# A spectral block with its gradients: the ScalarE order of one backward stage written down, two kinds of loads moved in their queue

## The chip, the cores and the metric

The kernel runs on one core of a Trainium2 chip. The metric is the device time of one execution in microseconds. A core has five engines that each run their own instructions in order: PE (TensorE, matrix products), DVE (VectorE), ACT (ScalarE), POOL (GpSimd) and SP (SyncE, which here only issues transfers). PEld is the loading of weights into PE. Transfers are issued by SP, by POOL, and run on 16 DMA engines that all issuers share.

## The reference

The forward pass takes x (2048 rows of 576 columns, bfloat16) and a condition c:

- six vectors `sa, ca, ga, sb, cb, gb` are cut from `silu(c) @ w_mod`;
- `h = layernorm(x) * (1 + ca) + sa`; `y = irfft2(rfft2(h) * (w_r + i w_i))`; `x1 = x + ga * y`;
- `h2 = layernorm(x1) * (1 + cb) + sb`; `out = x1 + gb * (((h2 @ w_gate) * (h2 @ w_up)) @ w_down)`, with 4608 hidden columns.

The outputs are `out` and the gradients of `sum(out * grad_out)` by x, w_r, w_i, w_gate, w_up, w_down, c and w_mod.

## The kernel before

Rows are dealt to 16 tiles of 128, hidden columns to 36 blocks of 128. The forward transform, the filter and the inverse transform come first, then one long loop over the 36 blocks that makes the products `g` and `u`, the gradient that flows back into `h2` (summed in `acc`) and the weight gradients. A weight gradient of one block and one half of the columns is a chain of 16 matmuls `u57p` (line 638) that ACT copies into `so` (line 640). The change lies behind this loop, in four stretches of the program:

- **The norm stage** (lines 940 to 1034), 16 tiles in four steps that overlap from tile to tile. `t1_norm` loads `n2c` and `yc` on SP, and by `norm_back` (lines 859 to 872) puts the gradient through the second layernorm: ACT makes `u` (line 862), DVE makes `w` from `n2c` (line 864) and the small sums `ab`, adds the residual to `u` (line 867) and gets `gxr` (line 872), `gxa` and `gxf` (lines 978 to 980). POOL stores `gxr`. `t1_turn` turns `gxf` on PE (line 985; called the turn below) and adds five column and diagonal sums that read `n2c` and `yc`, which frees these buffers. `t1_cols` and `t1_rows` are two more products each. ACT copies their results: `gyT` (line 987), `zt` (line 1005) and `b_Vp` (line 1013). These five results of a tile share three PSUM buffers.
- **The second stage** (lines 1119 to 1165), 19 groups of frequencies, with the filter gradients on DVE.
- **The third stage** (lines 1171 to 1225), 16 tiles: inverse transform and the first layernorm's backward, again by `norm_back`.
- **The output projection**, 1152 matmuls `u3p` (line 1269) of hidden activations `hl` with `w_down` (held in `wd0` to `wd4`). Rows go in eight pairs of tiles. A pair needs four loads `hl` of 576 KB, numbered 0 to 31 over all pairs. Their buffers are six slots in turn, except for numbers 24 to 27 (pair 6), which have a pool `hlp` of their own that is laid where the third stage's buffers were. Behind tiles 8 to 13 stands a `section` each (line 922): a vector is spread by PE (`spp`, line 913), copied and scaled by ACT (`dmb`, `o8`, lines 925 and 932), `wmj` is loaded and `o8` stored on SP, and DVE takes five products `pr7` (line 938).

**What sets the order.** The library orders each engine's instructions by priorities and by what it expects to be ready, and places waits where data or buffers ask for them. Two tools overrule it: `in_order` chains instructions of one engine, and `tc.issue_after` (through `behind`) puts one behind another. `deal` (line 874) writes PE's order from the end of the long loop to the end of the third stage. It puts the pieces of the three stages in a row, and after each piece some fillers out of one list: the last 144 weight gradient products (`held`), then the `u3p` products of the first five pairs (`proj`, 720 of them). A step of the norm stage gets 16 fillers, of the second stage 12, of the third stage 20 in its first step and then 16. ACT's order in these stages isn't written down. SP's order in the norm stage is written in part (lines 1023 to 1026): the late stores of weight gradients stand behind chosen loads of `n2c`.

SP issues in its order. A transfer that waits holds all later ones of SP.

Of the kernel before, what the change touches and what calls it, by code (L numbers as in the profile page):

```python
# [10 lines left out]
BF = mybir.dt.bfloat16  # L11
# [8 lines left out]
NT = 16  # L20
S = 2048
D = 576
DP = 640
# [75 lines left out]
def build(ctx, tc, A_x, A_w_r, A_w_i, B_w_gate, B_w_up, B_w_down, c_in, w_mod, grad_out,  # L99
# [50 lines left out]

    def pe_since(mark):
        return [i for i in nc.cur_bb.bb.instructions[mark:] if i.engine == mybir.EngineType.PE]

    def in_order(seq):

# [422 lines left out]
    with ExitStack() as ms:  # L578
# [17 lines left out]
        with ExitStack() as bs:  # L596
# [31 lines left out]
            def u57_items(sf, rhs_n, done):  # L628
                so = so4[:, nso[0] % NSO, :]
                nso[0] += 1  # L630
                items = []
                for h in range(2):
                    pw = []

                    def item(h, t, pw=pw):
                        if t == 0:
                            pw.append(u57ps.tile([128, 512], FP32, name="u57p", tag="x"))
                        mm = nc.tensor.matmul(pw[0][:, 0:288], lhsT=sf[:, t, :], rhs=rhs_n(t, h * 288, 288), start=(t == 0), stop=(t == NT - 1))  # L638
                        if t == NT - 1:
                            nc.scalar.copy(so[:, h * 288:(h + 1) * 288], pw[0][:, 0:288])  # L640
# [164 lines left out]
    with ExitStack() as ts:  # L805
# [47 lines left out]
        def behind(insts):  # L853
# [2 lines left out]
                es.enter_context(tc.issue_after(i_))  # L856
            return es

        def norm_back(pool, gn, n, rstd, res, out, name):
            s12 = pool.tile([128, 2], FP32, name="s12" + name)  # L860
            u = pool.tile([128, D], BF, name="u" + name)
            nc.scalar.activation(out=u[:], in_=gn[:], func=ACT.Copy, scale=rstd, accum_out=s12[:, 0:1])
            w = pool.tile([128, D], BF, name="w" + name, bufs=1)
            nc.vector.scalar_tensor_tensor(out=w[:], in0=gn[:], scalar=rstd, in1=n, op0=MUL, op1=MUL, accum_out=s12[:, 1:2])  # L864
            ab = pool.tile([128, 2], FP32, name="ab" + name)
            nc.vector.tensor_scalar(out=ab[:], in0=s12[:], scalar1=-1.0 / D, scalar2=None, op0=MUL)
            nc.vector.tensor_tensor(out=u[:], in0=u[:], in1=res, op=ADD)
            if name == "1":
                nc.scalar.activation(out=w[:], in_=n, func=ACT.Identity, bias=ab[:, 0:1], scale=ab[:, 1:2])  # L869
            else:  # L870
                nc.vector.tensor_scalar(out=w[:], in0=n, scalar1=ab[:, 1:2], scalar2=ab[:, 0:1], op0=MUL, op1=ADD)
            return nc.vector.tensor_tensor(out=out, in0=u[:], in1=w[:], op=ADD)
# [12 lines left out]
        def wide(m):  # L885
            return slice(m * 128, (m + 1) * 128)
# [53 lines left out]
        with ExitStack() as r1:  # L940
# [3 lines left out]
            csA = ps_cs.tile([128, 512], FP32, name="csA")  # L944
            csB = ps_cs.tile([128, 512], FP32, name="csB")
            csC = ps_cs.tile([128, 512], FP32, name="csC")
            rings = {k: c1b.tile([128, n, DP], BF, name=k) for k, n in (("gxr", 4), ("gxf", 2))}
            ga_h = c1b.tile([128, D], BF, name="ga_h")
            gxa = c1b.tile([128, D + 4], BF, name="gxa")
            with tc.high_priority(HEAD_START):  # L950
                for k in rings:
                    nc.vector.memset(rings[k][:, :, D:DP], 0.0)
                nc.vector.memset(gxa[:, D:D + 4], 0.0)
            ld, gyTs, zts = {"order": []}, {}, {}

            def t1_norm(t):
                if t == 0:
                    nc.sync.dma_start(ga_h[:], modb_d[:, MGA, :])
                for k, src in (("n2c", n2_d), ("yc", y_d)):
                    ld[k, t] = c1.tile([128, D], BF, name=k, bufs=5 if k == "n2c" else 4)  # L960
                    with behind(ld["order"]):
                        ins = nc.sync.dma_start(ld[k, t][:], src[:, t, :])
                    ld[k, "ins", t] = ins.ins
                if t in (1, 2):
# [12 lines left out]
                gf = rings["gxf"][:, t % 2, :]  # L977
                nc.vector.tensor_tensor(out=gxa[:, 0:D], in0=gx, in1=ga_h[:], op=MUL)
                nc.vector.tensor_tensor(out=gf[:, 0:DF], in0=gxa[:, 0:DF], in1=gxa[:, D:DF - 2:-1], op=ADD)
                nc.vector.tensor_tensor(out=gf[:, DF:D], in0=gxa[:, 1:DF - 1], in1=gxa[:, D - 1:DF - 1:-1], op=SUB)  # L980

            def t1_turn(t):
                pt = ps_fp.tile([128, 5, 128], BF, name="trp", tag="fp")
                for m in range(5):
                    nc.tensor.transpose(pt[:, m, :], rings["gxf"][:, t % 2, wide(m)], ident[:])
                gyTs[t] = c1z.tile([128, 5, 128], BF, name="gyT")
                nc.scalar.copy(gyTs[t][:], pt[:])
# [11 lines left out]
            def t1_cols(t):  # L999
                zt = zts[t] = c1z.tile([128, 2, FP], BF, name="zt")  # L1000
                for cc in range(2):
                    zp = ps_fp.tile([128, 512], FP32, name="zp", tag="fp")
                    for m in range(3):
                        nc.tensor.matmul(zp[:, :FP], lhsT=gyTs[t][:, 2 * cc + m, :], rhs=T["RF"][:, 3 * cc + m, :], start=(m == 0), stop=(m == 2))
                    nc.scalar.copy(zt[:, cc, :], zp[:, :FP])

            def t1_rows(t):
                zt = zts[t]
                for cc in range(2):
                    vp = ps_fp.tile([128, 512], FP32, name="vp", tag="fp")  # L1010
                    nc.tensor.matmul(vp[:, :FP], lhsT=T["G1"][:, t, 0, :], rhs=zt[:, cc, :], start=True, stop=False)
                    nc.tensor.matmul(vp[:, :FP], lhsT=T["G1"][:, t, 2 if cc == 0 else 1, :], rhs=zt[:, 1 - cc, :], start=False, stop=True)
                    nc.scalar.copy(Vv[:, :, t, cc, :], vp[:, :FP].rearrange("k (g f) -> k g f", f=4))

            steps = [t1_norm, t1_turn, t1_cols, t1_rows]
            for k in range(NT + len(steps) - 1):
# [230 lines left out]
        late = {8: (MSB, of_sums(dsb)), 9: (MCB, of_rows(dcb)), 10: (MGA, of_rows(dga)), 11: (MGB, of_rows(dgb)), 12: (MSA, of_sums(dsa)), 13: (MCA, of_rows(dca))}  # L1247


        proj = []  # L1250
        for tp_ in range(NT // 2):
            hls = [first_hl[q] if tp_ == 0 else hl_load(4 * tp_ + q, behind_=ld["yc", "ins", NT - 1]) for q in range(4)]
            x1t = o2p.tile([128, 2, D], BF, name="x1t3")
            with behind([last[nc.gpsimd]] if tp_ == 0 else []):
                x1l = nc.gpsimd.dma_start(x1t[:], x1_d[:, 2 * tp_:2 * tp_ + 2, :])
# [3 lines left out]
            for group in [[(0, 0), (1, 0)], [(0, 1), (1, 1)]] if tp_ == 0 else [[(0, 0)], [(0, 1)], [(1, 0)], [(1, 1)]]:  # L1259
# [5 lines left out]
                        obs[ti] = o2p.tile([128, D], BF, name="ob3", bufs=4)  # L1265
                for fb in range(NFB):
                    f0, w = wd_part(fb)
                    for ti, h in group:
                        mm = nc.tensor.matmul(p2[ti][:, 0:288], lhsT=hls[fb // 9][:, fb % 9, ti * 128:(ti + 1) * 128], rhs=w[:, fb - f0, h * 288:(h + 1) * 288], start=(fb == 0), stop=(fb == NFB - 1))  # L1269
                for ti, h in group:  # L1270
                    nc.scalar.copy(obs[ti][:, h * 288:(h + 1) * 288], p2[ti][:, 0:288])
# [90 lines left out]
```

## Time and profile before

| what | value |
|---|---|
| median of three runs | 1550.34 us (1549.38 to 1552.56) |
| the profiled execution, and its span | 1548.15 us, 1546.4 us |
| PE, DVE, ACT, POOL busy | 97%, 69%, 38%, 15% of the span |
| end of the long loop and first norm tiles, 1254 to 1275 us | PE busy 18.11 of 21.00 us, DVE 20.91 |
| norm stage, 1275.00 to 1324.12 us | PE busy 38.65 of 49.12 us, DVE 34.09, ACT 27.81, granted clock 0.97 |
| rest of it, 1324.12 to 1348 us | PE busy 23.88 of 23.88 us |
| second stage, 1348 to 1404 us | PE busy 56.00 of 56.00 us, DVE 48.53, ACT 45.85 |
| third stage, 1404 to 1470.4 us | PE busy 66.13 of 66.40 us, DVE 53.37, ACT 45.31 |

Start and end times of matmuls are modelled, so "busy" says that PE had work, not that it worked at its peak. The granted clock is the share of its full rate that PE was given. A row of a timeline gives the start, the length, the engine, the line, the operation with its tiles, and how many were merged; behind it, in brackets, how long the engine had idled and what ended that. A group of n merged matmuls lasts n spacings and the length of the last one. T1 is below the start of the turn of tile 1, and so on; S is the end of PE's part in the third stage.

### The profile page before, as it was taken

How to read it: one execution, taken by the hardware profiler on the slowest of the kernel's cores; microseconds unless marked ns; L12 is line 12 of the kernel's file. 1: busy time of each engine (PE TensorE's matmuls, PEld its weight loads, DVE VectorE, ACT ScalarE, POOL GpSimd, SP SyncE). 2: the span in 40 equal slices, each digit the busy share in tenths (PEclk: the TensorE clock that was granted, in tenths of full speed). 3: DMA queues.
4: the chain of work that ended last, by engine and by line, in shares of the span. 5: the costliest groups of instructions: out<-in, count | busy, mean ns of one | idle time of the engine just before them, and what ended most of it. 6: DMA issues, size and time to landing. Idle time of an engine off the chain costs nothing.

```text
span 1546.4 us, 29006 instructions
## 1 busy us (share of the span) xinstructions
PE 1495.4 (97%) x11144; PEld 1013.4 (66%) x11144; DVE 1060.0 (69%) x2647; ACT 582.4 (38%) x1189; POOL 237.2 (15%) x360
## 2 busy tenths in 40 slices
PE   6999989999999999999999999999999997999987
PEld 4666533566666666666676666766667665888765
DVE  6866643666667766677676676766767686488883
ACT  6667732322222222222222222222222225586752
POOL 0001212111101111111110110211111022221022
PEclk9999999999999999999999999999999999999999
DMA  8968997587868768778687686876877688856685
GB/s 315 286 202 226 263 269 216 141 171 151 180 122 167 148 123 165 148 149 170 121 165 149 142 158 139 155 168 128 163 143 147 120 207 237 275 186 195 191 296 156
DMA packets 487181, 280.42 MB, mean 181 GB/s; under 512 B 408865, under 2 KB 457378, under 8 KB 486018
## 3 DMA queue, kind: packets, MB, share of 16 engines
q1 hardware_dynamic: 458882, 175.32, 54.4%
q0 software_dynamic: 28160, 103.25, 23.0%
q8 instruction: 87, 1.43, 0.4%
q14 instruction: 52, 0.43, 0.1%
HBM read 108.62 MB, written 82.31 MB: 123 GB/s over the span
## 4 chain that ended last, share of the span: by engine, by line
PE 83%; DVE 8%; DMA 4%; ACT 3%; issue 2%; SPq 0%; POOL 0%; POOLq 0%; DVEq 0%; ACTq 0%
PE u57p L638 26%; PE u8p L741 18%; PE gup L705 16%; PE u4p L446 7%; PE u3p L1269 5%; PE gup L700 3%; DMA xc<-in_A_x_dram 2%; DVE w L864 1%; DMA n2c<-n_d 1%; DMA hl<-hhT_d 1%; PE zp L385 1%; DVE ln_st L176 1%; ACT w L869 1%; PE u4p L441 1%; DVE goT L417 1%
## 5 line engine op out<-in xcount | busy, mean ns | idle before, releaser
L746 DVE TENSOR_TENSOR acc<-acc,u8p 128x288 f32<-128x288 f32 (+1 forms) x1088 | 483.0, 452 | 276.4 <-PE u8p L741 272.8
L741 PE MATMUL u8p<-wT,ggT 128*128 128x288 bf16 x1152 | 328.4, 287 | 2.9 <-DVE acc L746 2.9
L741 PE MATMUL u8p<-wT,guT 128*128 128x288 bf16 x1152 | 328.0, 286 | 0.0
L705 PE MATMUL gup<-h2T,wgu 128*128 128x512 bf16 x1152 | 298.0, 380 | 0.0
L640 ACT CAST so<-u57p 128x288 bf16<-128x288 f32 x216 | 85.9, 398 | 519.1 <-PE u57p L638 511.7
L638 PE MATMUL u57p<-h2p,gu_sf 128*128 128x288 bf16 x1152 | 187.0, 287 | 0.0
L638 PE MATMUL u57p<-h2p,gg_sf 128*128 128x288 bf16 x1152 | 186.0, 286 | 0.0
L1269 PE MATMUL u3p<-wd,hl 128*128 128x288 bf16 x1152 | 172.2, 293 | 7.7 <-DMA hl<-hhT_d 6.9
L705 PEld LDWEIGHTS <-wgu 128*128 128x128 bf16 x1152 | 109.4, 98 | 98.0 <-issue 17.1
L741 PEld LDWEIGHTS <-ggT 128*128 128x128 bf16 x1152 | 112.4, 98 | 66.7 <-issue 14.0
L446 PE MATMUL u4p<-goT,wdT 128*128 128x512 bf16 x656 | 151.3, 380 | 3.2 <-DVE ghh_st L168 2.6
L741 PEld LDWEIGHTS <-guT 128*128 128x128 bf16 x1152 | 112.6, 98 | 58.9 <-issue 3.6
L707 ACT CAST gT<-gup 128x512 bf16<-128x512 f32 x144 | 84.3, 585 | 131.6 <-PE gup L705 129.7
L1269 PEld LDWEIGHTS <-hl 128*128 128x128 bf16 x1152 | 109.1, 100 | 36.1 <-DMA hl<-hhT_d 7.9
L638 PEld LDWEIGHTS <-gu_sf 128*128 128x128 bf16 x1152 | 112.5, 98 | 28.9
L638 PEld LDWEIGHTS <-hh_sf 128*128 128x128 bf16 x1152 | 112.6, 98 | 28.5
L638 PEld LDWEIGHTS <-gg_sf 128*128 128x128 bf16 x1152 | 112.3, 98 | 28.4
L707 ACT CAST uT<-gup 128x512 bf16<-128x512 f32 x144 | 84.3, 586 | 77.6 <-PE gup L705 77.6
L446 PEld LDWEIGHTS <-wdT 128*128 128x128 bf16 x656 | 61.2, 98 | 75.5 <-issue 10.2
L638 PE MATMUL u57p<-gonC,hh_sf 128*128 128x288 bf16 x576 | 99.7, 286 | 0.0
L718 POOL DMA_DIRECT2D hhT_d<-hhT x36 | 33.2, 922 | 375.4 <-DVE hhT L709 352.6
L168 DVE CAST ghh_st<-u4p 128x512 bf16<-128x512 f32 x56 | 38.7, 690 | 59.1 <-PE u4p L446 59.0
(373 smaller groups left out, 1839.9 us busy)
## 6 DMA issues: line engine op xcount, KB each, us to landing
ghhT_d<-ghh_st POOLq DMA_DIRECT2D x36, 512.0 KB, 4.0
ghh<-ghhT_d POOLq DMA_DIRECT2D x36, 512.0 KB, 7.9
hhT_d<-hhT POOLq DMA_DIRECT2D x36, 512.0 KB, 6.3
hl<-hhT_d SPq DMA_DIRECT2D x28, 576.0 KB, 5.7
out_dram<-woT SPq DMA_DIRECT2D x70, 128.0 KB, 2.0
wdn<-in_B_w_down_dram SPq DMA_DIRECT2D x18, 288.0 KB, 3.8
wd<-in_B_w_down_dram POOLq DMA_DIRECT2D x36, 144.0 KB, 4.9
out_dram<-so SPq DMA_DIRECT2D x36, 144.0 KB, 2.8
```

Of the source, the lines that this page charges most:

```text
L168: nc.vector.tensor_copy(dst, src)
L176: nc.vector.bn_stats(out=st[:, t, h, :], in_=xt[:, t, h * 288:(h + 1) * 288])
L446: nc.tensor.matmul(pt[:], lhsT=wdTs[k][:, j, m, :], rhs=goT[:, 4 * sb4:4 * sb4 + 4, m, :], start=(m == 0 and n == 5), stop=(m == n - 1))
L638: mm = nc.tensor.matmul(pw[0][:, 0:288], lhsT=sf[:, t, :], rhs=rhs_n(t, h * 288, 288), start=(t == 0), stop=(t == NT - 1))
L640: nc.scalar.copy(so[:, h * 288:(h + 1) * 288], pw[0][:, 0:288])
L700: nc.tensor.matmul(pts[-1][:], lhsT=wgu[r, 8, jw * 128:(jw + 1) * 128], rhs=h2T[r, 4 * sb4:4 * sb4 + 4, 4, :], start=True, stop=False)
L705: nc.tensor.matmul(pts[k][:], lhsT=wgu[:, 4 * wi_ + m, jw * 128:(jw + 1) * 128], rhs=h2T[:, ts_, m, :], start=False, stop=(m == 3))
L707: nc.scalar.copy((gT, uT)[wi_][:, th_, :], pts[k][:])
L718: nc.gpsimd.dma_start(hhT_d[:, :, fb, :].rearrange("tp f x -> f tp x"), hhT[:].rearrange("f (tp ti) p -> f tp (ti p)", ti=2))
L741: nc.tensor.matmul(pu[:, 0:288], lhsT=l_, rhs=r_, start=(k == 0), stop=(k == len(mms) - 1))
L746: summed[t] = nc.vector.tensor_tensor(out=ghb(t)[:, hs_] if fbs[-1] == NFB - 1 else dst, in0=dst, in1=pu[:, 0:288], op=ADD).ins
L1269: mm = nc.tensor.matmul(p2[ti][:, 0:288], lhsT=hls[fb // 9][:, fb % 9, ti * 128:(ti + 1) * 128], rhs=w[:, fb - f0, h * 288:(h + 1) * 288], ...
```

## The change

1. **ACT's order in the norm stage.** `followed` notes for a matmul which ACT copy evacuates it. While `deal` writes PE's order, it also lists ACT's copies of the norm stage and of the fillers in it, in the order of their matmuls, and puts the `u` of tile k+2 at the end of step k (the turn of step k is that of tile k-1). `in_order` then chains them. So `u` of tile t stands behind the copy `gyT` of tile t-3, and, while weight gradient fillers last, behind that step's `so`. Before, the library had it behind `gyT` of tile t-6.
2. **Loads.** `n2c` is asked for one tile further ahead than `yc`; `yc` has three buffers for four. SP's order keeps its shape: `n2c` of tile t is still the load that waits for the turn of tile t-5; beside it stands now `yc` of tile t-2 where `yc` of tile t-1 stood.
3. **Buffers.** `gxf` has a ring of three for two, `gxr` loses its padding (and its memset goes), `gb_h` gets a pool of its own between `wd4` and the last left slot of `hl`. Addresses behind it move by 1152 bytes.
4. **Third stage.** 14 fillers for 16 in each step but the first.
5. **Last pairs.** The loads `hl` of pairs 5 and 6 are asked for with those of pair 4, and those of pair 7 in two halves with pairs 5 and 6. SP's order in the built program: 22 and 23 at the third stage's end, 24 to 27 right behind, all ahead of the sections' transfers; 28 and 29 behind the second section's stores, 30 and 31 behind the fourth's. Before, 24 stood behind the first section's stores, 25 to 27 behind the fourth section's load, 28 and 29 behind the sixth's, 30 and 31 behind the fifth's stores.

PE's order is the same up to the third stage. There it has 244 fillers instead of 272, and the 28 come behind the stage. DVE's order in the norm stage becomes regular (a tile's `gxa` and `gxf` directly behind the next tile's `w`), and in the last stretch the filter gradients come ahead of all `pr7`. POOL loads `wd4` ahead of the store of `gxr` 11 instead of behind it.

```diff
+    then_act = {}
+
+    def followed(mm, act):
+        then_act[mm.ins.name] = act.ins
...
-                            nc.scalar.copy(so[:, h * 288:(h + 1) * 288], pw[0][:, 0:288])
+                            followed(mm, nc.scalar.copy(so[:, h * 288:(h + 1) * 288], pw[0][:, 0:288]))
...
         wd_pool(28, 8)
+        gbhp = pool("gbhp", 1)
         hl_pool("left", ts)
...
-            nc.scalar.activation(out=u[:], in_=gn[:], func=ACT.Copy, scale=rstd, accum_out=s12[:, 0:1])
+            scaled[name].append(nc.scalar.activation(out=u[:], in_=gn[:], func=ACT.Copy, scale=rstd, accum_out=s12[:, 0:1]).ins)
...
         def deal(held, proj):
-            more, seq = held + proj, list(lead)
+            more, seq, acts = held + proj, list(lead), scaled["2"][0:3]
             for n, (stage, k, ins) in enumerate(staged):
+                last_ = len(seq)
                 seq += ins
                 steps = sum(x[:2] == (stage, k) for x in staged)
                 at = sum(x[:2] == (stage, k) for x in staged[:n + 1])
-                q = 16 if stage == 1 else 12 if stage == 2 else 20 if k == 0 else 16
+                q = 16 if stage == 1 else 12 if stage == 2 else 20 if k == 0 else 14
                 q = q * at // steps - q * (at - 1) // steps
                 seq, more = seq + more[:q], more[q:]
+                if stage == 1:
+                    acts += [then_act[i_.name] for i_ in seq[last_:] if i_.name in then_act]
+                    acts += scaled["2"][k + 2:k + 3] * (at == steps and k > 0)
             in_order(seq)
+            in_order(acts)
...
-            rings = {k: c1b.tile([128, n, DP], BF, name=k) for k, n in (("gxr", 4), ("gxf", 2))}
+            rings = {k: c1b.tile([128, n, w], BF, name=k) for k, n, w in (("gxr", 4, D), ("gxf", 3, DP))}
...
-                for k, src in (("n2c", n2_d), ("yc", y_d)):
-                    ld[k, t] = c1.tile([128, D], BF, name=k, bufs=5 if k == "n2c" else 4)
+                for k, src, tt in [("n2c", n2_d, 0)] * (t == 0) + [("n2c", n2_d, t + 1)] * (t < NT - 1) + [("yc", y_d, t)]:
+                    ld[k, tt] = c1.tile([128, D], BF, name=k, bufs=5 if k == "n2c" else 3)
                     with behind(ld["order"]):
-                        ins = nc.sync.dma_start(ld[k, t][:], src[:, t, :])
-                    ld[k, "ins", t] = ins.ins
+                        ins = nc.sync.dma_start(ld[k, tt][:], src[:, tt, :])
+                    ld[k, "ins", tt] = ins.ins
...
-            gb_h = modh(MGB, "gb_h", tl, nc.gpsimd)
+            gb_h = modh(MGB, "gb_h", gbhp, nc.gpsimd)
...
-        proj = []
+        proj, hls_of = [], {0: first_hl}
         for tp_ in range(NT // 2):
-            hls = [first_hl[q] if tp_ == 0 else hl_load(4 * tp_ + q, behind_=ld["yc", "ins", NT - 1]) for q in range(4)]
+            for nq in {4: range(16, 28), 5: (28, 29), 6: (30, 31)}.get(tp_, range(4 * tp_, 4 * tp_ + 4) if 0 < tp_ < 4 else ()):
+                hls_of.setdefault(nq // 4, []).append(hl_load(nq, behind_=ld["yc", "ins", NT - 1]))
+            hls = hls_of[tp_]
```

The copies of `gyT`, `zt`, `b_Vp` and of the projection's results are wrapped in `followed` in the same way as that of `so`.

More of the change, by code (lines that the diff above doesn't have):

```diff
@@ L857, in behind @@
             return es
+        scaled = {"1": [], "2": []}
         def norm_back(pool, gn, n, rstd, res, out, name):
@@ L950, in build @@
             with tc.high_priority(HEAD_START):
-                for k in rings:
-                    nc.vector.memset(rings[k][:, :, D:DP], 0.0)
+                nc.vector.memset(rings["gxf"][:, :, D:DP], 0.0)
                 nc.vector.memset(gxa[:, D:D + 4], 0.0)
@@ L976, in t1_norm @@
                 ld["gx", t] = nc.gpsimd.dma_start(gx1_d[:, t, :], gx).ins
-                gf = rings["gxf"][:, t % 2, :]
+                gf = rings["gxf"][:, t % 3, :]
                 nc.vector.tensor_tensor(out=gxa[:, 0:D], in0=gx, in1=ga_h[:], op=MUL)
@@ L984, in t1_turn @@
                 for m in range(5):
-                    nc.tensor.transpose(pt[:, m, :], rings["gxf"][:, t % 2, wide(m)], ident[:])
+                    mm = nc.tensor.transpose(pt[:, m, :], rings["gxf"][:, t % 3, wide(m)], ident[:])
                 gyTs[t] = c1z.tile([128, 5, 128], BF, name="gyT")
-                nc.scalar.copy(gyTs[t][:], pt[:])
+                followed(mm, nc.scalar.copy(gyTs[t][:], pt[:]))
                 gh, gx = ghb(t), rings["gxr"][:, t % 4, :]
@@ L1003, in t1_cols @@
                     for m in range(3):
-                        nc.tensor.matmul(zp[:, :FP], lhsT=gyTs[t][:, 2 * cc + m, :], rhs=T["RF"][:, 3 * cc + m, :], start=(m == 0), stop=(m == 2))
-                    nc.scalar.copy(zt[:, cc, :], zp[:, :FP])
+                        mm = nc.tensor.matmul(zp[:, :FP], lhsT=gyTs[t][:, 2 * cc + m, :], rhs=T["RF"][:, 3 * cc + m, :], start=(m == 0), stop=(m == 2))
+                    followed(mm, nc.scalar.copy(zt[:, cc, :], zp[:, :FP]))
             def t1_rows(t):
@@ L1011, in t1_rows @@
                     nc.tensor.matmul(vp[:, :FP], lhsT=T["G1"][:, t, 0, :], rhs=zt[:, cc, :], start=True, stop=False)
-                    nc.tensor.matmul(vp[:, :FP], lhsT=T["G1"][:, t, 2 if cc == 0 else 1, :], rhs=zt[:, 1 - cc, :], start=False, stop=True)
-                    nc.scalar.copy(Vv[:, :, t, cc, :], vp[:, :FP].rearrange("k (g f) -> k g f", f=4))
+                    mm = nc.tensor.matmul(vp[:, :FP], lhsT=T["G1"][:, t, 2 if cc == 0 else 1, :], rhs=zt[:, 1 - cc, :], start=False, stop=True)
+                    followed(mm, nc.scalar.copy(Vv[:, :, t, cc, :], vp[:, :FP].rearrange("k (g f) -> k g f", f=4)))
             steps = [t1_norm, t1_turn, t1_cols, t1_rows]
@@ L1267, in build @@
                     f0, w = wd_part(fb)
+                    mms = []
                     for ti, h in group:
                         mm = nc.tensor.matmul(p2[ti][:, 0:288], lhsT=hls[fb // 9][:, fb % 9, ti * 128:(ti + 1) * 128], rhs=w[:, fb - f0, h * 288:(h + 1) * 288], start=(fb == 0), stop=(fb == NFB - 1))
-                for ti, h in group:
-                    nc.scalar.copy(obs[ti][:, h * 288:(h + 1) * 288], p2[ti][:, 0:288])
+                        mms.append(mm)
+                for (ti, h), mm in zip(group, mms):
+                    followed(mm, nc.scalar.copy(obs[ti][:, h * 288:(h + 1) * 288], p2[ti][:, 0:288]))
                 proj += pe_since(mark) if tp_ < 5 else []
```

## The prediction

> **What bounds the kernel now.** I read the busy shares first, then the windows of the four stretches behind the long loop, then PE's waits there, and then the timelines of the engines that the waits name.
>
> ```profile
> PE zp L1004 <- ACT b_Vp L1013: 8.6, 5, 3.3
> PE u3p L1269 <- DMA hl<-hhT_d: 6.9, 3, 4.0
> ```
>
> PE is the bound almost everywhere, so only what PE loses counts. The waits (us, times, longest) from 1272 us on name two losses: `zp` in the norm stage waits 8.6 us for ACT's copy `b_Vp`, and `u3p` behind the stages waits 6.9 us for `hl`. The first, step by step from PE's timeline (starts of the turns T1, T5, T6, T8, T10, T11):
>
> ```profile
> 1272.69 0.44 PE L985 MATMUL trp<-ident,gxf 128*128 128x128 bf16 x5
> ...
> 1297.69 0.44 PE L985 MATMUL trp<-ident,gxf 128*128 128x128 bf16 x5
> ...
> 1302.27 0.44 PE L985 MATMUL trp<-ident,gxf 128*128 128x128 bf16 x5
> ...
> 1315.12 0.44 PE L985 MATMUL trp<-ident,gxf 128*128 128x128 bf16 x5
> ...
> 1324.12 0.44 PE L985 MATMUL trp<-ident,gxf 128*128 128x128 bf16 x5
> ...
> 1328.36 0.44 PE L985 MATMUL trp<-ident,gxf 128*128 128x128 bf16 x5
> ```
>
> A step that nothing holds up takes 4.24 us (1324.12 to 1328.36). The nine from T1 to T10 take 51.43, against 9 x 4.24 = 38.16; 0.37 of the 13.3 more is three extra fillers in the first step, so 12.9 us are lost. How, shows in one step on DVE, ACT and PE:
>
> ```profile
> 1304.37 0.82 DVE L864 SCALAR_TENSOR_TENSOR w<-gn,rstd2g,n2c 128x576 bf16<-128x576 bf16 x1 [3.12 <-DMA n2c<-n_d]
> ```
> ```profile
> 1307.63 0.77 ACT L862 ACTIVATE u<-gn,rstd2g 128x576 bf16<-128x576 bf16 x1 [4.13 <-DVE gxr L872]
> ```
> ```profile
> 1309.13 0.53 PE L1004 MATMUL zp<-T_RF,gyT 128*128 128x292 bf16 x3 [3.33 <-ACT b_Vp L1013]
> ```
>
> It is a ring. A turn frees a buffer of `n2c`; the load goes out; DVE has idled 3.12 us for it; only then come `gxr` and, through the buffer of `u`, the `u` six tiles on, for which ACT has idled 4.13 us. The `b_Vp` copies stand behind that `u` on ACT, though their data are long there; `zp` needs their PSUM buffer and waits 3.33 us; the next turn stands behind `zp`.
>
> The second loss, the stretch behind the third stage (window columns: PE, PEld, DVE, ACT, POOL, clock):
>
> ```profile
> 1470.40:1541.10 70.70, 63.77 (x454) 47.73 (x453) 40.98 (x109) 31.31 (x57) 18.14 (x29) 0.90 0.79 243
> ...
> 1497.30:1506.60 9.30, 9.26 (x56) 6.52 (x57) 3.30 (x13) 0.45 (x2) 4.03 (x7) 0.73 1.06 351
> ```
> ```profile
> 1497.34 9.18 PE L1269 MATMUL u3p<-wd,hl 128*128 128x288 bf16 x54 [4.03 <-DMA hl<-hhT_d]
> 1506.35 1.14 PE L913 MATMUL spp<-dsa,sel 128*128 128x288 f32 x4
> 1507.32 8.98 PE L1269 MATMUL u3p<-wd,hl 128*128 128x288 bf16 x72
> ...
> 1523.74 17.33 PE L1269 MATMUL u3p<-wd,hl 128*128 128x288 bf16 x117 [0.70 <-DMA hl<-hhT_d]
> ```
>
> 72 products take 8.98 us, a spacing of (8.98 - 0.29)/71 = 0.1224. Of the window's 454 matmuls 432 are `u3p`: 52.9 us at that spacing; 20 are `spp`, in five fours of 0.97 (1506.35 to 1507.32): 4.85. That makes 57.7 of 70.7; 13.0 are lost. The waits for `hl` are 6.9. Another 5.2 is slow clock right behind them: 54 products take 9.18 (53 x 0.1224 + 0.29 = 6.78) at a clock of 0.73, and 117 take 17.33 instead of 14.49. 0.8 stays unnamed.
>
> **The change part by part.**
>
> *Norm stage.* In the new order `u` of tile t stands behind `gyT` of tile t-3, not t-6, and DVE's order is regular. The step T5 to T6 of before happens to have nearly the new pattern, so it prices what stays. On ACT and PE:
>
> ```profile
> 1299.90 0.77 ACT L862 ACTIVATE u<-gn,rstd2g 128x576 bf16<-128x576 bf16 x1 [0.98 <-DVE gxr L872]
> 1300.58 0.19 ACT L862 ACTIVATION_READ_ACCUMULATOR u<-gn,rstd2g 128x1 f32 x1
> 1300.68 0.38 ACT L640 CAST so<-u57p 128x288 bf16<-128x288 f32 x1
> 1300.95 0.71 ACT L1013 CAST b_Vp<-vp 128x292 bf16<-128x292 f32 x2
> ```
>
> `u` and `so` still go ahead of `b_Vp`; that step took 4.58, so 0.34 more than 4.24. Seven steps keep such a pattern: 7 x 0.34 = 2.4 stay, and 12.9 - 2.4 = **10.5 us go** (bounds 0 and 12.9). This needs the loop open: gradient work on DVE and the loads must be done within the lead that is left.
>
> ```profile
> 1312.24:1316.90 4.66, 3.93 (x42) 3.13 (x40) 3.52 (x10) 3.17 (x8) 0.53 (x1) 1.00 0.62 187
> ```
> ```profile
> DMA to landing us min/median/max: 2.1/4.3/9.3
> ```
> ```profile
> DMA to landing us min/median/max: 2.2/5.2/10.9
> ```
>
> DVE is busy 3.52 us of a step and ACT 3.17, both under 4.24. The two landing rows are those of `n2c` and of `yc`, from issue. A load of `n2c` has four steps from the turn that frees its buffer to the turn that needs it: 18.3 us at 4.58, less 1.1 for the sums and the issue and 3.5 for DVE's work behind it, leaves 13.7 for a landing of at most 9.3. `yc`, with one buffer less, has three steps, 13.7 less 0.7, for at most 10.9. Both are covered; if the cover fails, every step pays the difference.
>
> *`wd4`.* Its load, with its wait, follows the last transposed weight gradients that SP moves:
>
> ```profile
> 1318.98 1.23 SPq L650 DMA_TRANSPOSE wo_l<-so  x1
> ```
> ```profile
> 1322.63 0.90 POOL L1051 DMA_DIRECT2D wd<-in_B_w_down_dram  x1 [4.38 <-DMA wo_l<-so]
> ```
> ```profile
> wd<-in_B_w_down_dram POOLq DMA_DIRECT2D x1, 1152.0 KB, 6.7
> ```
> ```profile
> 1329.38 1.15 PE L1269 MATMUL u3p<-wd,hl 128*128 128x288 bf16 x8
> ```
>
> Before, the load goes out 7.5 us behind T8 (1315.12) and lands 6.7 later, at T8 + 14.2, where the first product that reads it starts (T8 + 14.26). Undisturbed, PE wants it at T8 + 13.74: **+0.5 us** (bounds 0 and 4.7, the latter if it takes the 10.9 us of the slowest load). POOL puts it ahead of the store of `gxr` 11, which then waits too; the ring of four hides that. The moved addresses, the third buffer of `gxf` and the memset that goes touch no engine that PE waits for: 0.
>
> *Third stage.* DVE's and PE's timelines, two steps:
>
> ```profile
> 1444.92 0.46 DVE L872 TENSOR_TENSOR ob<-u,w 128x576 bf16<-128x576 bf16 x1 [0.58 <-ACT w L869]
> ...
> 1448.68 0.46 DVE L872 TENSOR_TENSOR ob<-u,w 128x576 bf16<-128x576 bf16 x1 [0.57 <-ACT w L869]
> ```
>
> DVE's step is 3.76 us with its own wait for ACT, and none for PE between these rows. PE, at 16 fillers, just fills it. With 14 PE has 3.76 - 2 x 0.1224 = 3.51 us of work, so I let it idle 0.25 a step; the stage does not get shorter, and 28 products run behind it: 28 x 0.1224 = **+3.4 us** (bounds 0, if PE had set the step after all, and 3.4).
>
> *Behind the stages.* S is PE's end of the third stage, 1470.4 before. The landing of `hl`, from issue, from 1460 us on:
>
> ```profile
> DMA to landing us min/median/max: 3.8/7.6/11.5
> ```
>
> In the new order 24 to 27 go out by about S + 3 and are wanted at S + 23; 28 and 29 go behind the second section, about S + 13, wanted at S + 42; 30 and 31 behind the fourth, about S + 28, wanted at S + 45. Each has more than 11.5. So the waits (6.9) and the slow clock behind them (5.2) go: -12.2 with rounding (bounds 0 and -13.0). Late next are 22 and 23. The buffer of 22 is freed by product 693 of 1152, which is now the first behind the stage; it goes out at S + 0.5 and is wanted 28 + 18 products and one `spp` later, at S + 6.6; 23 goes at S + 2.3 and is wanted at S + 7.7. At the median of 7.6 they hold PE 1.5 and 0.7 us, at 3.8 nothing, at 11.5 5.4 and 0.7. I take 1.0, as fewer other transfers run at that point than in the middle of the sections: **-11.2 us** together.
>
> **Sum:** -10.5 + 0.5 + 3.4 - 11.2 = -17.8. The profiled execution took 1548.15, 2.2 below the median of 1550.34; it goes to 1530.3, the median to **1532.5 us**.
>
> **The rivals.**
>
> *The norm stage keeps its loss.* Loads, not ACT, would set its step: with `yc` in three buffers and both loads in one queue, a wait at the head of SP holds the other. The 3.12 us of DVE above, which a load ended, speak for it; the slack of 13.7 against 9.3, and of 13.0 against 10.9, speaks against it. 10.5 us more: 1543.0.
>
> *The tail keeps its waits.* Six loads of 576 KB go out together at S. At the 351 GB/s of the window above, 3.5 MB take 10 us, and 22 and 23 could share the queues with the four that nobody wants yet; the gain is given back through S + 13. Queues that serve in order of issue speak against it. 11.2 us more: 1543.7.
>
> *Slower: the clock falls.* The new order trades one long stall for a short idle in each step, 0.25 us in the third stage and 0.34 in the norm stage. If the granted clock then fell to the 0.73 seen behind the 4.03 us wait, the third stage would pay 16 x (3.51/0.73 - 3.76) = 16.8 us and eight norm steps 8 x 4.24 x (1/0.73 - 1) = 12.5, 29.3 against a gain of 17.8: 1561.8. It decides from a clock of about 0.80 downward in both stages (90.1/c - 94.1 = 17.8). Against it:
>
> ```profile
> 1300.00:1310.00 10.00, 6.50 (x61) 5.02 (x60) 4.88 (x14) 5.41 (x15) 1.55 (x2) 1.00 1.10 237
> ```
>
> Here PE was busy 6.50 of 10 us and the clock stayed at 1.00. The Trainium skill describes this rival: on the page "TensorE: Matmul & The Clock Gate", section "A second HAM failure mode: psum-queue depth-cycling", a kernel that hands PSUM buffers round idles briefly between groups of products, often enough that the clock swings between half and full. By that rule the trade would be a bad one, at half clock worse than the price above; the row just quoted does not show it, the row at 0.73 shows only what follows a long wait for data.
>
> *Nothing is gained.* Another engine or queue takes the place of ACT, and the loads come no earlier in fact than in the list; then only the costs are left, +3.9 us: 1554.2, or less if they don't come either.
>
> **How the numbers follow.** Forecast 0.52 (1524 to 1538 with the bounds of its terms), norm stage 0.16, tail 0.14, clock 0.12, nothing 0.06. About 0.2% (3.1 us) is what a measurement of this kernel can tell from no change. The first three are faster: 0.82. Of the last, half is within it: 0.03; with the clock, slower is 0.15. The low end, 1524, is the forecast with every term at its good bound: the third stage's 3.4, the 1.0 of late `hl`, the norm stage's 2.4, `wd4`'s 0.5 and the tail's unnamed 0.8 are all gone (1532.5 - 8.1). The high end, 1546, takes in the second and third case, with half of the way to `wd4`'s bad bound on top (1543.7 + 2.1).
>
> **What would show it.** In the profile of the changed kernel: turns T2 to T10 some 4.3 to 4.6 us apart and the wait of `zp` for `b_Vp` under 2.5 us in sum; no DVE idle over 1 us for `n2c`; `wd4` holding the first product of the fifth part by about 0.5 us; `ob` of the third stage still 3.76 us apart; 460 products behind it, with waits for `hl` of about 1 us, all before S + 10, and no window at 0.73. I am wrong if DVE idles for `n2c` or `yc` in each step, if PE's step in the third stage falls to 3.5, if the waits for `hl` come back at S + 23, or if the granted clock of the two stages is below 0.95.

## The result, and the profile after

The changed kernel takes 1541.95 us (median of 13 runs, 1532.64 to 1550.00), the kernel before 1548.73 on the same chips (13 runs, 1544.42 to 1553.70). The ratio of the runs is 0.9953, 95% interval 0.9931 to 0.9976: faster, by 6.8 us between the medians, and by 3.7 to 10.7 in the interval. The forecast was 17.8.

The profiled execution took 1535.20 us, 12.95 less than that of before. Part of this is not the change's. The first products of the long loop start 3.4 us earlier, in code that the change doesn't touch; from the tile view of `gup` of the kernel before and of the changed one (count, shortest, median and longest in ns, first and last start):

```profile
L705 PE MATMUL gup<-h2T,wgu x176: 378/379/391, 278.7 to 399.1; 128*128 128x512 bf16 x176
```
```profile
L710 PE MATMUL gup<-h2T,wgu x176: 378/379/390, 275.3 to 395.7; 128*128 128x512 bf16 x176
```

In the profiles of all kernels below this start lies between 274 and 287 us, though no edit touches what comes ahead of it. I therefore compare the stretch from T1 to PE's last product (its start, E), and its parts, from PE's timelines; S in the table is the start of PE's last row of the third stage. The column behind that is the rest of the span, from E on. Each ratio comes from all runs of the kernel and of the one before beside it, the times from one profiled execution:

| kernel | T1 to T10 | T10 to T12 | T15 to S | S to E | T1 to E | behind E | ratio to before (95%) |
|---|---|---|---|---|---|---|---|
| before | 51.43 | 8.48 | 124.62 | 70.74 | 268.22 | 5.5 | |
| changed | 40.88 | 14.19 | 124.59 | 66.25 | 258.88 | 5.5 | 0.9953 (0.9931 to 0.9976) |
| e1, ScalarE's order, loads, buffers | 40.89 | 20.17 | 124.63 | 69.12 | 267.77 | 5.5 | 0.9953 (0.9929 to 0.9978) |
| e2, early `hl` alone | 52.65 | 8.47 | 124.62 | 65.09 | 263.79 | 5.6 | 1.0000 (0.9976 to 1.0025) |
| e3, transposes first | 40.89 | 13.04 | 124.61 | 66.70 | 258.20 | 5.5 | 0.9954 (0.9926 to 0.9981) |
| e4, 16 fillers | 40.89 | 11.00 | 124.62 | 61.42 | 250.89 | 9.2 | 0.9948 (0.9925 to 0.9971) |
| e5, smaller stores | 40.90 | 14.56 | 124.89 | 64.84 | 258.15 | 5.1 | 0.9922 (0.9897 to 0.9947) |
| e6, `wmj` first | 40.89 | 16.48 | 124.59 | 61.49 | 256.42 | 5.5 | 0.9923 (0.9897 to 0.9949) |
| e7, `pr7` first | 40.89 | 14.88 | 124.59 | 63.71 | 257.03 | 6.9 | 0.9940 (0.9895 to 0.9986) |
| e8, loads unshifted | 40.88 | 17.79 | 124.59 | 67.08 | 263.30 | 5.5 | 0.9959 (0.9933 to 0.9984) |
| e9, `wd4` elsewhere | 40.88 | 8.48 | 124.60 | 66.04 | 252.97 | 5.5 | 0.9927 (0.9907 to 0.9947) |
| e10, e4 + e6 + e9 | 40.88 | 9.51 | 124.63 | 57.99 | 245.97 | 6.6 | 0.9897 (0.9872 to 0.9923) |

The changed kernel's stretch is 9.3 us shorter, which is inside the interval of the runs; 17.8 is not. Behind E, POOL stores the last results. That rest is 5.1 to 5.6 us, but 9.2 in e4, 6.9 in e7 and 6.6 in e10, so some of what these three gain up to E is lost behind it.

**The norm stage** does what was forecast. PE's waits from 1240 us on in the changed kernel:

```profile
PE u3p L1284 <- DMA wd<-in_B_w_down_dram: 3.9, 1, 3.9
PE u3p L1284 <- ACT ob L1287: 2.8, 1, 2.8
PE u8p L746 <- DVE acc L751: 2.3, 2, 2.0
PE zp L1016 <- ACT b_Vp L1025: 1.2, 7, 0.2
```

The wait of `zp` for `b_Vp` is now seven times some 0.18 us instead of five times up to 3.3. From T1 to T10 DVE waits for `n2c` once, 0.3 us. The turns T2, T3, T8, T9 and T11, T12 on PE's timeline, with the row that matters between the last two:

```profile
1273.99 0.44 PE L997 MATMUL trp<-ident,gxf 128*128 128x128 bf16 x5
...
1278.57 0.44 PE L997 MATMUL trp<-ident,gxf 128*128 128x128 bf16 x5
...
1301.45 0.44 PE L997 MATMUL trp<-ident,gxf 128*128 128x128 bf16 x5
...
1305.69 0.44 PE L997 MATMUL trp<-ident,gxf 128*128 128x128 bf16 x5
...
1314.17 0.44 PE L997 MATMUL trp<-ident,gxf 128*128 128x128 bf16 x5
...
1319.31 2.08 PE L1284 MATMUL u3p<-wd,hl 128*128 128x288 bf16 x8 [3.94 <-DMA wd<-in_B_w_down_dram]
...
1324.12 0.44 PE L997 MATMUL trp<-ident,gxf 128*128 128x128 bf16 x5
```

Steps take 4.58 us while `so` and `u` stand ahead of `b_Vp`, then 4.24. From T11 to T12 a step takes 9.95: PE waits 3.94 us for `wd4`, and then eight products take 2.08 us instead of 1.15. The granted clock is the last but two of these columns; behind the wait it is 0.65:

```profile
1319.30:1324.12 4.82, 4.82 (x26) 3.20 (x26) 0.18 (x1) 1.41 (x4) 0.00 (x0) 0.65 0.06 21
```

So `wd4` costs 5.71 us, 9.95 less the 4.24 of an undisturbed step. Why it is late shows on SP's and POOL's timelines:

```profile
1295.37 1.95 SPq L655 DMA_TRANSPOSE wo_l<-so  x1
...
1302.42 0.32 SPq L974 DMA_DIRECT2D n2c<-n_d  x1
1302.83 0.38 SPq L974 DMA_DIRECT2D yc<-y_d  x1
1305.14 0.40 SPq L662 DMA_DIRECT2D out_dram<-wo_l  x1
1305.58 0.51 SPq L663 DMA_DIRECT2D out_dram<-wo_l  x1
1306.19 1.83 SPq L655 DMA_TRANSPOSE wo_l<-so  x1
```
```profile
1311.34 0.90 POOL L1063 DMA_DIRECT2D wd<-in_B_w_down_dram  x1 [8.43 <-ACT gyT L999]
```
```profile
wd<-in_B_w_down_dram POOLq DMA_DIRECT2D x1, 1152.0 KB, 7.9
```

The landings of the first transposed transfer, from the view of transfers, in the changed kernel and before:

```profile
wo_l<-so SPq DMA_TRANSPOSE x1, 9.7
```
```profile
wo_l<-so SPq DMA_TRANSPOSE x1, 5.2
```

It goes out at 1295.37 and lands 9.7 us later. Its store (1305.14) waits for it at the head of SP, and the second transposed transfer (1306.19), whose data ACT had written by 1299.5, stands behind that store. That one lands 4.5 us later, at 1310.7. `wd4` lies on the memory that it reads; so the load goes out at 1311.34, T8 + 9.9, and lands 7.9 us later, at T8 + 17.8, where PE wants it at T8 + 13.74. (The releaser that POOL's row names is inferred, and is no part of this chain.)

**The third stage** keeps its length with 14 fillers (124.59 from T15 to S, 124.62 before); the inverse transform of a step on PE still starts 3.76 us after that of the step before, and the granted clock is 1.00 from 1404 to 1460 us:

```profile
1445.80 0.92 PE L1208 MATMUL yp<-T_IF,ut 128*128 128x289 bf16 x6
...
1449.56 0.92 PE L1208 MATMUL yp<-T_IF,ut 128*128 128x289 bf16 x6
```

**Behind it** no product waits for `hl` any more. But one waits for `ob`, ACT's copy that frees the PSUM buffer. PE, ACT, DVE and SP of the changed kernel:

```profile
1485.14 1.13 PE L926 MATMUL spp<-dgb,ones_f 128*128 128x288 f32 x4
1489.04 10.65 PE L1284 MATMUL u3p<-wd,hl 128*128 128x288 bf16 x72 [2.77 <-ACT ob L1287]
1499.53 1.13 PE L926 MATMUL spp<-dsa,sel 128*128 128x288 f32 x4
1500.50 8.98 PE L1284 MATMUL u3p<-wd,hl 128*128 128x288 bf16 x72
```
```profile
1484.27 0.70 ACT L938 COPY dmb<-spp 128x288 f32<-128x288 f32 x2 [8.32 <-DVE pr L951]
1485.00 3.56 ACT L945 ACTIVATE o<-dmb,sc_col 128x576 bf16<-128x576 f32 x5
1488.59 0.70 ACT L1287 CAST ob<-u3p 128x288 bf16<-128x288 f32 x2
```
```profile
1479.96 0.76 DVE L951 SCALAR_TENSOR_TENSOR pr<-wmj,dmb 128x576 bf16<-128x576 bf16 x1 [1.42 <-DMA wmj<-in_w_mod_dram]
```
```profile
1463.80 2.86 SPq L1063 DMA_DIRECT2D hl<-hhT_d  x5
1466.75 0.86 SPq L940 DMA_DIRECT2D wmj<-in_w_mod_dram  x1
1467.66 0.53 SPq L941 DMA_DIRECT2D wmj<-in_w_mod_dram  x1
```

Read from the bottom: `wmj` of the first section goes out behind six loads `hl` and is there at 1479.96, over 12 us later (S is 1461.68, so that is S + 18.3); DVE's first `pr7` waits for it; the `pr7` of two sections hold both buffers of `dmb`; ACT idles 8.32 us for one, then makes `dmb` and `o8`, and the `ob` copies stand 4.3 us behind that; PE waits 2.77 us. The 72 products behind that take 10.65 instead of 8.98. That makes 4.4 us (2.77 + 1.67).

### The profile page after: what moved, and what is told of

The parts are those of the page before. It is cut to its first block, busy times and chain, and to the rows that moved or that the text cites. A ratio compares the mean times of both kernels' runs of the same rounds, so it can differ in the third digit from the quotient of the medians.

```text
span 1533.4 us, 29027 instructions
## 1 busy us (share of the span) xinstructions
PE 1494.3 (97%) x11140; PEld 1012.6 (66%) x11144; DVE 1060.9 (69%) x2646; ACT 582.5 (38%) x1189; POOL 237.3 (15%) x360
## 5 line engine op out<-in xcount | busy, mean ns | idle before, releaser
L451 PEld LDWEIGHTS <-wdT 128*128 128x128 bf16 x656 | 61.2, 98 | 74.0 <-issue 8.7
```

Source lines behind the costliest of these rows:

```text
L451: nc.tensor.matmul(pt[:], lhsT=wdTs[k][:, j, m, :], rhs=goT[:, 4 * sb4:4 * sb4 + 4, m, :], start=(m == 0 and n == 5), stop=(m == n - 1))
```

## The experiments

Each is an edit of the changed kernel, but for e2.

**e1: ScalarE's order, loads of the norm stage and buffers alone.** The loop over pairs asks for `hl` as before, and `14` is `16`.

```diff
-            for nq in {4: range(16, 28), 5: (28, 29), 6: (30, 31)}.get(tp_, ...):
-                hls_of.setdefault(nq // 4, []).append(hl_load(nq, behind_=ld["yc", "ins", NT - 1]))
-            hls = hls_of[tp_]
+            hls = [first_hl[q] if tp_ == 0 else hl_load(4 * tp_ + q, behind_=ld["yc", "ins", NT - 1]) for q in range(4)]
```

> Parts 1 to 3 alone: ScalarE's order, the loads of the norm stage and the buffers as in the changed kernel; the loads hl and the 16 fillers of the third stage as before. Theory A (the norm stage's gain is real, and half of it is given back at the first product that reads wd4): the turns T1 to T10 lie 40 to 42 us apart (51.4 before, 40.9 changed), u3p waits 3 to 5 us for wd4 behind T11, and the stretch behind the third stage has its waits for hl of about 7 us again; 4 to 7 us below the kernel before. Rival B (the norm stage was only quick in the one traced execution): T1 to T10 is 45 us or more here.

Measured: T1 to T10 40.89, so the gain of the norm stage is no chance of one trace. In the profiled execution, the slowest of its twelve, `u3p` waited 8.14 us for `wd4`, not 3 to 5, and the step before 1.96 us for `yc`; T10 to T12 took 20.17, and the whole gain was given back (267.77 against 268.22). Over all its runs the ratio to before is 0.9953, and the medians differ by 5.6 us, as expected. So this execution isn't typical, and the price of `wd4` is not the same in every trace. It follows the first transposed transfer: that landed 14.1 us after its issue here. Over the profiles with SP's order as changed, landing and wait are 8.3 and 2.36 (e4), 8.9 and 3.09 (e5), 8.9 and 3.40 (e7), 9.7 and 3.94 (changed), 10.7 and 5.80 (e6), 11.9 and 7.71 (e8), 14.1 and 8.14 (e1).

**e2: the early loads `hl` alone, in the kernel before.**

> Part 5 alone, in the kernel before: the loads hl of the last pairs ahead of the sections, 16 fillers. VectorE's products pr7 come behind the filter gradients here too. Theory A: the norm stage is as before (51 us from T1 to T10, no wait for wd4 over 1 us); behind the third stage no wait for hl over 1 us, but ACT's copies ob are late by 2 to 4 us once, so that the stretch from the last turn of the third stage takes 63 to 64 us where it took 71; 6 to 9 us below the kernel before. Rival B (six early loads hl only crowd the queues): waits for hl of 22 and 23 or for other loads of over 4 us, and 0 to 3 us below.

Measured: S to E 65.09, 5.7 less than before; no wait for `hl` 22 or 23, one of 2.38 us for a later `hl`, and 2.62 us in which `spp` waited for ACT's `dmb`. The traced stretch is 4.4 us shorter, but the ratio is 1.0000, 0.24% (3.7 us) to both sides: by time this run shows no gain. That is less than theory A's 6 to 9 us; rival B's 0 to 3 us fits, but not its waits of over 4 us. What the trace of one execution gained here, the runs as a whole don't confirm. The same shows in the whole change: with e1 and the changed kernel both at 0.9953, the moved loads `hl` and the 14 fillers together bring nothing that the runs can tell, though their intervals, some 0.24% to each side, don't exclude the 4.5 us that the trace of the changed kernel gains from S to E.

**e3: the last transposed transfer ahead of the store that held it.**

```diff
-            for t, k in zip((5, 6, 7, 9, 9, 11, 11, 13, 13, 15), (0, 1, 3, 4, 5, 6, 7, 8, 9, 10)):
+            for t, k in zip((5, 6, 7, 9, 9, 11, 11, 12, 13, 15), (0, 1, 3, 4, 5, 6, 7, 9, 8, 10)):
```

> The changed kernel; on SP the last transposed weight gradient goes behind the load n2c 12, ahead of the store that it stood behind, which waited for the transfer before it. Theory A (the load of wd4 is late because its transposed store was held in SP's order): the load of wd4 goes out by T8 + 6 instead of T8 + 9.9, u3p waits under 1.5 us for it, T11 to T12 takes 4.2 to 6 us instead of 9.95; 3 to 6 us below the changed kernel. Rival B (the transfers are late because the norm stage now moves the same bytes in 10 us less): the load goes out or lands as late as before and the time is that of the changed kernel within 2 us.

Measured: 2.76 us of wait, T10 to T12 13.04 instead of 14.19. Theory A's 3 to 6 us didn't come. SP's and POOL's rows of this kernel (T8 is 1302.00):

```profile
1301.02 2.01 SPq L655 DMA_TRANSPOSE wo_l<-so  x1
```
```profile
1311.07 0.90 POOL L1063 DMA_DIRECT2D wd<-in_B_w_down_dram  x1 [7.61 <-DMA yc<-y_d]
```

The transfer went out 5.7 us earlier against T8 and landed 9.2 us after its issue instead of 4.5, so the load left at T8 + 9.1. SP's order was not enough of the cause. Rival B puts it down to the same bytes in less time; e5 was to test that.

**e4: 16 fillers.** The `14` in `deal` is `16`.

> The changed kernel with 16 fillers in each step of the third stage, as before. Theory A (VectorE and ScalarE set the third stage's step at 3.76 us, so that two fillers less only move 28 products behind it): the step stays at 3.76, the stretch behind the stage is 3.4 us shorter, 3 to 4 us below the changed kernel. Rival B (TensorE set the step): the step grows from 3.5 to 3.75 and the time stays within 1 us.

Measured: T15 to S 124.62, so theory A holds for the stage: 28 products fit into it for nothing. S to E is 4.8 us shorter, 3.4 of it the 28 products, the rest another stall (2.46 us, `spp` for `dmb`, in place of 2.77 and its slow clock); the changed kernel, e3, e5, e8 and e9 have the same orders behind S, and their S to E runs from 64.84 to 67.08, so that rest is no finding. But the program ends 9.2 us behind E and not 5.5: POOL's store of the last `of` stands behind four stores of the filter gradients, goes out at E + 3.3 instead of E + 1.9, and the span ends 5.9 us behind it instead of 3.6. So in this trace 3.7 of the 4.8 us are lost at the end, and the ratio (0.9948) doesn't tell this kernel from the changed one; the 3 to 4 us that theory A names for the whole are not shown. `wd4`'s wait was 2.36 us in this execution.

**e5: fewer bytes in the norm stage.**

```diff
-                ld["gx", t] = nc.gpsimd.dma_start(gx1_d[:, t, :], gx).ins
+                few = slice(0, 8) if 2 <= t < 10 else slice(0, 128)
+                ld["gx", t] = nc.gpsimd.dma_start(gx1_d[few, t, :], rings["gxr"][few, t % 4, 0:D]).ins
...
-                nc.sync.dma_start(ld3[k][:], src[:, sa, :])
+                nc.sync.dma_start(ld3[k][:], src[:, 1 if k == "gxc" and 2 <= sa < 10 else sa, :])
```

> The changed kernel with less to move in the norm stage: of the stores gx_d of tiles 2 to 9 only 8 of 128 rows are written (1.1 MB less), and the third stage reads tile 1's instead; the values of those tiles are left out. Theory B (from the run with the transposed stores moved ahead: the load of wd4 is late because the DMA engines are full once the norm stage is 10 us shorter): the DMA share of the 11 us ahead of that load falls below 1.0, the transposed stores land in under 5 us, the load goes out by T8 + 7 and u3p waits under 1.5 us for it; T10 to T12 takes 8.5 to 10 us instead of 14.2. Theory A (only SP's order holds it): the wait stays at 2.4 to 4 us.

Measured: a wait of 3.09 us, T10 to T12 14.56, the load at T8 + 9.3. But the run doesn't decide. The DMA share (last but one column) did not fall; ahead of the load it is 1.13, where the changed kernel has 1.08, and the kernel before 0.80 and 0.71 in the same phase:

```profile
1299.20:1309.90 10.70, 10.54 (x110) 8.65 (x108) 9.64 (x28) 7.57 (x21) 0.55 (x2) 1.00 1.13 231
```
```profile
1300.00:1311.30 11.30, 11.15 (x117) 9.18 (x115) 10.07 (x30) 8.16 (x22) 0.55 (x1) 1.00 1.08 245
```
```profile
1304.00:1314.00 10.00, 5.94 (x56) 4.59 (x55) 7.36 (x21) 4.84 (x13) 0.53 (x1) 1.00 0.80 210
1314.00:1322.60 8.60, 8.60 (x89) 7.12 (x87) 6.25 (x19) 4.91 (x12) 1.08 (x2) 1.00 0.71 195
```

Nor was much of it cut: the stores of tiles 8 and 9 were short, but the one that goes out inside this window, tile 10's, is whole here too. What fills the engines stays open.

**e6: `hl` 24 to 27 behind the `wmj` of the first two sections.**

```diff
+            wmj_ins[j] = nc.sync.dma_start(wmj[64:128, 4, :], ...).ins
...
-            for nq in {4: range(16, 28), ...
+            for nq in {4: range(16, 24), ...
...
+                    if t == 9:
+                        for nq in range(24, 28):
+                            hls_of.setdefault(nq // 4, []).append(hl_load(nq, behind_=wmj_ins[late[9][0]]))
```

> The changed kernel with the loads hl 24 to 27 behind the loads wmj of the first two sections instead of ahead of them. Theory C (behind the third stage the six early loads crowd the queues, wmj lands 12 us after its issue, pr7 and with it ACT's dmb and ob come late): the first pr7 starts by S + 12 instead of S + 18.3, u3p's wait of 2.8 us for ob and the slow clock behind it go, S to the end takes 61 to 63 us instead of 66.3. Theory V (VectorE's order, filter gradients first): only as far as VectorE's order changes with it.

**e7: filter gradients behind the `pr7` of their tile, loads as changed.**

```diff
-                with tc.issue_after(ld3["last"]):
+                with tc.issue_after(pr_ins[late[t][0]]):
                     filter_grad(ci)
```

> The changed kernel with the filter gradients of the last stretch behind the products pr7 of the section of their tile, on VectorE; the loads as in the changed kernel. Theory V (VectorE's order makes pr7 late): the first pr7 starts by S + 12, the wait for ob goes, S to the end takes 61 to 63 us. Theory C (wmj lands late): the first pr7 still starts at S + 17 to 19 with VectorE idle ahead of it, and S to the end stays at 65 to 68 us.

These two tell the causes of the late `ob` apart. DVE's first `pr7` in e6 (S is 1475.44) and in e7 (S is 1461.98):

```profile
1485.84 0.76 DVE L953 SCALAR_TENSOR_TENSOR pr<-wmj,dmb 128x576 bf16<-128x576 bf16 x1 [1.71 <-DMA wmj<-in_w_mod_dram]
```
```profile
1479.39 0.76 DVE L953 SCALAR_TENSOR_TENSOR pr<-wmj,dmb 128x576 bf16<-128x576 bf16 x1 [2.79 <-DMA wmj<-in_w_mod_dram]
```

With `pr7` first on DVE it still starts at S + 17.4, with DVE idle for `wmj`, and `ob` is still 2.05 us late. With `wmj` ahead of four of the six loads on SP it starts at S + 10.4, no wait is left behind S, and S to E is 61.49, which is what 460 products and five `spp` need (61.2). Theory C holds: the loads in front of `wmj` were the cause, and moving four of them behind it was enough. In e6 DVE's order changes too, so a share of the 4.8 us may be that. Alone it brought 2.5 in e7 (63.71, under theory C's 65 to 68 and above V's 61 to 63), hardly more than the 2.2 us between kernels with the same orders behind S, and e7 ends 6.9 us behind E instead of 5.5.

**e8: the loads and rings of the norm stage as before, ScalarE's order as changed.**

```diff
-                for k, src, tt in [("n2c", n2_d, 0)] * (t == 0) + [("n2c", n2_d, t + 1)] * (t < NT - 1) + [("yc", y_d, t)]:
-                    ld[k, tt] = c1.tile([128, D], BF, name=k, bufs=5 if k == "n2c" else 3)
+                for k, src, tt in [("n2c", n2_d, t), ("yc", y_d, t)]:
+                    ld[k, tt] = c1.tile([128, D], BF, name=k, bufs=5 if k == "n2c" else 4)
```

> The changed kernel with the loads of the norm stage and its rings as before (n2c asked for with yc of the same tile, yc in four buffers, gxf in two): of the norm stage only ScalarE's order stays. Theory A (the written order of ScalarE opens the ring, the shift of n2c only adds slack): T1 to T10 stays at 40 to 42 us. Rival (without the shift the loads or the two buffers of gxf set the step): T1 to T10 takes 44 to 50 us, with DVE waiting for n2c or TensorE's turn for gxf.

Measured: 40.88. The written order of ScalarE is enough to open the ring; the shift of `n2c` and the third buffer of `gxf` bring nothing here. (`wd4`'s wait was 7.71 us in this execution.)

**e9: `wd4` on other memory.**

```diff
-        hl_pool("left", ts)
         wd_pool(28, 8)
+        hl_pool("left", ts)
         gbhp = pool("gbhp", 1)
+        pool("gapl", 1).tile([128, 160], BF, name="gapl")
         hl_pool("left", ts)
...
-                hl = hlt[(0, 3, 4, 1, 2, 5)[slot[0] % 6]].tile([128, 9, 256], BF, name="hl")
+                hl = hlt[(0, 3, 4, 2, 1, 5)[slot[0] % 6]].tile([128, 9, 256], BF, name="hl")
```

> The changed kernel; only addresses differ: wd4 lies ahead of the memory of the last transposed weight gradients (so4) instead of on it, the second slot of hl and gb_h lie on it, and the slot of hl 3 behind it. The load of wd4 then waits for earlier stores and for TensorE's last weight gradient product, not for the two last transposed transfers. Theory A2 (that wait alone makes wd4 late): the load goes out at T8 + 1 to T8 + 4 instead of T8 + 9 to 12, lands ahead of T8 + 13.7, u3p's wait for wd4 is 0, T10 to T12 takes 8.5 us instead of 13 to 20. Theory B (the DMA engines are full whatever the order): the load goes out early but lands 12 us or more later, and the wait stays at 2 us or more.

POOL's row, the landing of this load, and T8 on PE in this kernel:

```profile
1304.87 0.90 POOL L1064 DMA_DIRECT2D wd<-in_B_w_down_dram  x1 [1.55 <-DMA wo_l<-so]
```
```profile
wd<-in_B_w_down_dram POOLq DMA_DIRECT2D x1, 1152.0 KB, 8.5
```
```profile
1301.86 0.44 PE L998 MATMUL trp<-ident,gxf 128*128 128x128 bf16 x5
```

The load leaves at T8 (1301.86) + 3.0 and lands at T8 + 11.5, ahead of T8 + 13.7. T10 to T12 takes 8.48, as where nothing waits; the 5.7 us are back, and the ratio to before is 0.9927. A2 holds, but not to the letter. POOL's row still names a transposed transfer: the first one went out at 1295.77 and landed 9.0 us later, at 1304.77, and the load left 0.1 us behind that. So what the new place takes off is the wait for the second transfer alone; the load still hangs on the first. Its own landing takes 8.5 us against 7.9.

**e10: e4, e6 and e9 together.**

> The changed kernel with the three findings put together: wd4 laid elsewhere, 16 fillers in the third stage, hl 24 to 27 behind the first two sections' wmj. If each of the three costs is what the single runs showed (wd4 3 to 10 us, third stage 3.4 us, behind the stage 4 to 5 us) and they add, the stretch from T1 to the end takes 244 to 247 us, where the kernel before takes 268 and the changed one 259, and the median lies 12 to 18 us below the changed kernel's. Rival (a gain at one place is a wait at the next): 250 us or more.

Measured: 245.97 us from T1 to E, inside 244 to 247. S to E is 57.99, where 432 products and five `spp` need 57.7. The median is 1526.90 us, and the ratio to before 0.9897 (0.9872 to 0.9923), 1.0% where the changed kernel has 0.5%. By the two ratios that is some 9 us below the changed kernel, less than the 12 to 18 that I had set. Of the 12.9 us of the traced stretch 1.1 are lost behind E; why the runs move less than the rest stays open. The one wait in the stretch besides the 0.18 of `zp` is 0.86 us for `yc`, with its three buffers. It hides another: here the first transposed transfer took 12.6 us, `wd4` left at T8 + 6.2 and landed 8.4 us later, at T8 + 14.6, behind the T8 + 13.74 of a PE that nothing holds up.

## Why the forecast was half right

- **The norm stage, -10.5.** Right, mechanism and size: T1 to T10 fell by 10.55, the residue is 0.34 a step, and e1 and e8 repeat it. The rival in which the loads set the step is refuted for T1 to T10. Behind T10 PE waited for `yc` in two traces with three buffers, 1.96 us in e1 and 0.86 in e10, and in none with four (before, e2, e8); the forecast had that load covered.
- **`wd4`, +0.5 (bounds 0 and 4.7).** This step failed; it measured 5.7, and 2.5 to 9.6 over the profiles with SP's order as changed in which `wd4` lies where it did. I took "T8 + 7.5" for the issue and 6.7 us for the landing from the trace of before. There the two transposed transfers landed in 5.2 and 2.9 us, and nothing in their chain was late. In the shortened stage the chain of transfer, store, transfer, load sets the time: the first lands in 9.7 us, the second in 4.5. I had bounded the landing of the load, but not that of the transfers in front of it, and not the slow clock behind a wait, 1.8 us here. Another order on SP took little of it away (e3); another place, off the memory that the second transfer reads, took all of it away (e9).
- **Third stage, +3.4.** Right, by the trace: 14 fillers do not shorten it, and 16 cost nothing in it (e4).
- **Behind the stages, -11.2.** The waits for `hl` went, and 22 and 23 cost nothing instead of 1.0. This step failed too, in that nothing else was priced as late: I looked only at the loads that were moved, not at `wmj`, which they were moved past on SP. 4.4 us came back there. With 28 products more S to E fell by 4.5, where -11.2 + 3.4 = -7.8 was forecast. The rival with six loads crowding at S had the mechanism; it named `hl` 22 and 23 as the victims, and they were not.
- **Sum.** -10.55, +5.71, -4.49 and nothing else between T1 and E: -9.3 for -17.8. The two missed prices, 5.2 and 3.3, are the difference in this execution. The medians fell by 6.8; where the 2.5 us between them and the trace come from isn't shown.
- **The clock rival** is refuted as stated: with an idle of 0.18 us in seven steps of the norm stage, and with two fillers less in a step of the third, the clock stayed at 1.00 in both. A slow clock came, but behind single waits.
- Open is why the first transposed transfer takes 8.3 us in one execution and 14.1 in another. It took long in executions whose loop also started late (e1, e6, e8), but 12.6 us in e10 too, whose loop started as that of before. That full queues stretch it is argued, not shown: e5 did not lower the DMA share, and while the first transfer was under way the share was 0.96 before, where it took 5.2 us, 1.05 in the changed kernel and 1.07 in e1, where it took 9.7 and 14.1.

## What to carry to other kernels

When a stage is made shorter, list every load that is wanted inside it and follow its chain back over addresses, transfers and queue order; the times of that chain in the old trace were measured in a slower stage and are no prices for the new one. When transfers are moved ahead in a queue, price what they are moved past, and follow it to the engine in whose order an urgent copy stands behind it. A load with a deadline shouldn't be laid on memory that is freed last.

## What was not expected of the hardware

- A transposed transfer from SP of 128 by 640 values took from 2.6 to 14.1 us from issue to landing. The second of the two, asked for 5.7 us earlier against T8 (e3), took 9.2 us instead of 4.5, and landed 1 us earlier (T8 + 8.2 for T8 + 9.2).
- PE's clock fell behind waits of 2.8 to 8.1 us in the norm stage (to 0.65 behind 3.94), but the time lost behind the wait does not grow with it: 1.8 us behind 3.94, 3.0 behind 3.09 (e5), 1.4 behind 8.14 (e1), and 0.2 behind 2.36 (e4).
